# Half of the sequence-DFT sums made on the fly, other prepared sums moved to other units

## The chip, the core and the metric

The kernel runs on one core of one Trainium2 chip. A core has TensorE (PE, matrix products into PSUM), VectorE (DVE, elementwise), ScalarE (ACT, elementwise with a function), GpSimd (POOL) and SyncE (SP); each runs its own instructions in order, and they wait for each other by semaphores. SyncE and POOL also issue DMAs, which move data between the chip's memory (DRAM, here also used as scratch) and the on-chip pages. The metric is the time of one execution in microseconds of the device.

## The reference, cut to what matters

`x` is 2048 x 512, the sequence DFT matrices 2048 x 2048, the hidden ones 512 x 512, the gate and up weights 512 x 1792, the down weight 1792 x 512, all 32-bit floats.

```python
xn = _layernorm(x, axis=-1)
# FNet mixing, real part
a = einsum("bsd,ed->bse", xn, dft_hid_re)
b = einsum("bsd,ed->bse", xn, dft_hid_im)
s = einsum("ts,bse->bte", dft_seq_re, a) - einsum("ts,bse->bte", dft_seq_im, b)
# gated unit
h = sigmoid(xn @ w_gate) * (xn @ w_up)
g = silu(h @ w_down)
return x + s * g
```

## The kernel before, in words

**Products.** Each 32-bit operand is split into a hi part, rounded by ACT (line 67), and a lo part, the rest, by VectorE (line 68); a product is three matmuls, hi x hi, hi x lo, lo x hi (lines 71 to 73). Large products are made as 2 x 2 blocks in seven block products instead of eight, which needs sums and differences of the blocks ("sums" below) before and additions afterwards. The sums are VectorE operations recorded by one helper, `combine`, line 119.

**Order of work.** The program is a list of units, each a piece of TensorE work of some microseconds with the operands that it needs. A loop at the end (line 981 on) writes the instructions out unit by unit: the operations registered by `sooner(u, f)` ahead of unit u, the loads of the operands of units u to u+5 (`LOAD_AHEAD`), their splits for units u to u+2 (`SPLIT_AHEAD`), the unit's own work, then what `after(u, f)` registered. So the order on every engine and queue is fixed by unit numbers. All loads are issued by SyncE, nearly all stores by POOL. Data on the chip live in one pool of 53 pages of 4 KB per partition; a new page takes the place of one whose last use stands earlier in the program, and waits for that use.

**Stages.** The first half handles rows 0 to 1023 of `x`: a start, then blocks g = 1 to 6 of 256 hidden features each, nine units a block (`block_units`), units 0 to 53. The second half handles rows 1024 to 2047: block g = 0 in the same form (units 54 to 62), then six blocks in another form (`late_units`, seven units each). Then come the sequence DFT (`seq_units`) and the hidden DFT (`hidden_units`) with silu, product and addition of `x`. In the trace block 1 begins at 38.9 us, each block takes 30 to 31 us, the second half's first block begins at 222.2, the sequence DFT at 429.4, its four quarters of output rows at 429.4, 521.5, 597.7 and 673.8, the hidden DFT at 752.0.

**The sequence DFT.** A quarter has seven block products k in the order 1, 5, 6, 3, 7, 2, 4, each of four units pp = 0 to 3 with twelve matmuls of 512 columns. Units of this stage are numbered from its own start below (n in the code). Quarter 1 also carries eight small late down products of the gated unit, one behind every second unit, so it has units 0 to 35; quarter 2 has 36 to 63, quarter 3 has 64 to 91, quarter 4 has 92 to 119. The stationary operands are the blocks of `xn` (b11 etc. are the moving blocks of the DFT matrices, from `c_re` and `c_im`); split once in quarter 1, they stay on chip. Four of the moving operands of each pp are sums: t1 = b11 + b12 for k = 5, t2 = t1 + b22 for k = 6, t3 = b12 + b22 for k = 7, t4 = t2 + b21 for k = 4. In quarters 2 to 4 they are made during the quarter, the loads six units and the sum three units ahead of its use (line 844), in place in the block's page. In quarter 1 they are loaded from the scratch tensor `t_part`.

**Prepared sums.** `sums_ahead(n, make, blocks, to)` (line 675) loads four blocks ahead of units n and n+1 and, behind units n+3, n+5, n+6 and n+8, makes one sum each (VectorE, 128 x 1024) and stores it (POOL). It is used for
- `t_part`: the sums of quarter 1, pp = g - 1, in blocks g = 1 to 4 of the first half (line 961);
- `s_part`: differences of blocks of `xn`, rows 0 to 1023 in block 5 of the first half, rows 1024 to 2047 in the first block of the second half (line 963). `xn` itself is stored to `xn_part` as its row tiles are normalized; the last are stored behind unit 34;
- `w_part`: differences of the hidden DFT's weights `w_h`, from unit n+6 of the sequence DFT on (line 737).

**Silu ahead.** `silu_ahead(n, i)` (line 712), for i = 0 to 7, loads a page of the gated unit's output (`g_part` or `g_late`) ahead of unit n, makes the sigmoid on ACT behind unit n+2 (line 730), the product on VectorE behind n+3, and stores it to `gs_part`. The late down products end in accumulating stores to `g_late` (lines 460 and 462).

**After a product.** `snap` (line 795, ACT) copies a PSUM result out, `join` (line 802, VectorE) adds two, `two` makes four half-size sums of results, and POOL stores to `f_part`, which the hidden DFT reads.

Of the kernel before, what the change touches and what calls it, by code (L numbers as in the profile page):

```python
# [8 lines left out]
F32 = mybir.dt.float32  # L9
# [5 lines left out]
P = 128  # L15
S, D, F = 2048, 512, 1792
# [6 lines left out]
SB = 512  # L23
# [8 lines left out]
def fnet_glu_kernel(ctx: ExitStack, tc: tile.TileContext, x, c_re, c_im, w_h, w_gu, w_down, out):  # L32
# [6 lines left out]
    dram = ctx.enter_context(tc.tile_pool(name="dram", bufs=1, space=bass.MemoryType.DRAM))  # L39
# [21 lines left out]
    f_part = dram.tile([NT, 2, P, 8, SB], F32, name="f_part")  # L61
    w_part = dram.tile([4, P, 4, D // 2], F32, name="w_part")
    s_part = dram.tile([2, 4, P, 4, D // 2], F32, name="s_part")
    t_part = dram.tile([4, 4, P, 2, SB], F32, name="t_part")

    def split(hi, lo, src):
        nc.scalar.activation(hi, src, AF.Copy)  # L67
# [586 lines left out]
    def xn_blocks(q):  # L654
        a = {(d, j): Load(xn_part[q, j, d], [4, D // 2]) for d in range(2) for j in range(2)}
        return [a[k] for k in ((0, 0), (0, 1), (1, 0), (1, 1))]
# [76 lines left out]
    def seq_units(job):  # L733
        ops = a_operands()
        left = waiting + [(job, k) for k in SEVEN]
        n = len(units)
        sums_ahead(n + 6, diffs, [Load(w_h[i, j], [4, D // 2]) for i in range(2) for j in range(2)], w_part)
        for i in range(NS // 2):
            silu_ahead(n + 29 + 10 * i, i)
        for q in range(2):  # L740
            sooner(n - 5 + q, ops[1, q].load)
            sooner(n - 3 + q, ops[1, q].get)
        for tc_ in range(NT):
            n = len(units)
            bop = {}
            for pp in range(4):
                b11, b12, b21, b22 = c_blocks(tc_, pp)
                if tc_ == 0:
                    t1, t3, t2, t4 = (Load(t_part[pp, i], [2, SB]) for i in range(4))
                else:  # L750
                    t1 = Value([b11, b12], onto(b11.load, b12.load, ADD, nc.vector))
                    t2 = Value([b22], onto(t1.get, b22.load, ADD, nc.vector))
                    t3 = Value([b22], onto(b12.load, b22.load, ADD, nc.vector))
                    t4 = Value([b21], onto(t2.get, b21.load, ADD, nc.vector))
                bop[1, pp] = Parts([b11], b11.load, [2, SB])
                bop[5, pp] = Parts([t1], t1.get, [2, SB])
                bop[6, pp] = Parts([t2], t2.get, [2, SB])
                bop[3, pp] = Parts([b22], b22.load, [2, SB])
                bop[7, pp] = Parts([t3], t3.get, [2, SB])
                bop[2, pp] = Parts([b21], b21.load, [2, SB])  # L760
                bop[4, pp] = Parts([t4], t4.get, [2, SB])
                bop["t", pp] = {5: t1, 6: t2, 7: t3, 4: t4}
            ps, s, made = {}, {}, {}
            tags = {"a": "ab"[tc_ % 2], "b": "ba"[tc_ % 2], "c": "c"}

            def after_product(k, tc_=tc_, ps=ps, s=s, made=made):
                def halves(t):
                    return t.rearrange("p (h t) -> p h t", h=2)

                def put(blk):  # L770
                    half, j = blk // 2 ^ 1, blk % 2
                    nc.gpsimd.dma_start(f_part[tc_, half, :, 2 * j : 2 * j + 2, :], made[blk].rearrange("p h k t -> p h (k t)"))
                    if j == 0 or blk - 1 not in made:
                        return
                    (a0, a1), (b0, b1) = ([made[n][:, t, :, :].rearrange("p k t -> p (k t)") for t in range(2)] for n in (blk - 1, blk))
                    t1 = []

                    def two(i):
                        pg = page([2, SB], F32)
                        u, v = pg[:, 0, :], pg[:, 1, :]  # L780
                        if i == 0:
                            t1.append(combine(u, a0, a1, ADD))
                            combine(v, a1, b1, ADD)
                        else:
                            combine(u, t1[0], b1, ADD)
                            combine(v, u, b0, ADD)
                        nc.gpsimd.dma_start(f_part[tc_, half, :, 4 + 2 * i : 6 + 2 * i, :], pg)

                    after(now[0] + 1, lambda: two(0))
                    after(now[0] + 2, lambda: two(1))  # L790

                def snap(name, ch):
                    s[name] = page([2, 2, SB // 2], F32)
                    for d in range(2):
                        nc.scalar.activation(s[name][:, :, d, :], halves(ps[ch, d]), AF.Copy)
                    return s[name]

                def join(blk, name, ch, op, swap=False):
                    made[blk] = v = s[name]
                    for d in range(2):  # L800
                        x, y = v[:, :, d, :], halves(ps[ch, d])
                        nc.vector.tensor_tensor(v[:, :, d, :], *((y, x) if swap else (x, y)), op=op)
                    put(blk)

                if k == 1:
                    snap("u1", "a")
                elif k == 5:
                    snap("u5", "c")
                elif k == 6:
                    snap("u2", "a")  # L810
                elif k == 3:
                    join(2, "u2", "c", SUB)
                elif k == 7:
                    join(3, "u5", "a", SUB, swap=True)
                elif k == 2:
                    join(0, "u1", "b", ADD)
                else:
                    made[1] = snap("u4", "a")
                    put(1)

            CHAIN = {1: "a", 6: "a", 7: "a", 4: "a", 2: "b", 5: "c", 3: "c"}
            FIRST = (1, 2, 5)

            def run(k, pp, ops=ops, bop=bop, ps=ps, tags=tags, done=after_product):
                ch = CHAIN[k]
                if k in FIRST and pp == 0:
                    for d in range(2):
                        ps[ch, d] = bank("gu"[d] + tags[ch])
                wv, xv = ops[k, pp // 2].get(), bop[k, pp].get()
                for e in range(2):  # L830
                    o = 2 * (pp % 2) + e
                    for d in range(2):
                        ws = [t[:, o, d * P : (d + 1) * P] for t in wv]
                        first = k in FIRST and pp == e == 0
                        last = pp == 3 and e == 1
                        mm3(ps[ch, d], ws, [t[:, e, :] for t in xv], first, last, go_on=k not in FIRST)
                if pp == 3:
                    done(k)

            for k in ORDER:  # L840
                for pp in range(4):
                    m = len(units)
                    if tc_ and k in bop["t", pp]:
                        sooner(m - 6, bop["t", pp][k].load)
                        sooner(m - 3, bop["t", pp][k].get)
                    add([ops[k, pp // 2], bop[k, pp]], lambda k=k, pp=pp, run=run: run(k, pp))
                    if left and pp % 2:
                        last_down(*left.pop(0))
# [97 lines left out]
    with tc.manual_schedule():  # L946
# [3 lines left out]
        for h in range(NH):  # L950
            n = len(units)
            for g in range(NG):
                m = len(units)
                if h and g:
                    job = late_units(h, g, job)
                elif h:
                    job = block_units(h, g, job, [], Seven(g))
                elif g:
                    job = block_units(h, g, job, [])
                if h == 0 and 0 < g < 5:  # L960
                    sums_ahead(m, sums, c_blocks(0, g - 1), t_part[g - 1])
                elif (h, g) in ((0, 5), (1, 0)):
                    sums_ahead(m, diffs, xn_blocks(h), s_part[h])
            if h == 0:
                n = len(units)
                for i in range(KH):
                    m = 9 * (i // 2) + 6
                    if i % 2 == 0:
                        after(m - 6, lambda i=i: fetch(KH + i))
                    after(m - 4, lambda i=i: norm_a(KH + i))  # L970
                    after(m - 2, lambda i=i: norm_b(KH + i))
                    after(m, lambda i=i: (turn(KH + i), keep_raw(KH + i)))
                    after(m + 1, lambda i=i: store_xn(KH + i))
                for i, k in {-5: 1, -4: 2, 0: 6, 1: 5}.items():
                    sooner(n + i, xop[1, k].get)
                for i, k in {-3: 1, -2: 2, 1: 3, 2: 4}.items():
                    after(n + i, lambda k=k: x_sum(1, k))
            else:
                seq_units(job)
# [64 lines left out]
```

## Time and profile before

| | |
|---|---|
| median of three runs | 840.15 us (839.96 to 841.68) |
| the profiled execution | 840.49 us, span 838.6 us |
| TensorE busy | 822.7 us, 98% |
| VectorE busy | 656.9 us, 78% |
| ScalarE busy | 491.2 us, 59% |
| GpSimd busy | 145.6 us, 17% |
| DMA | 216.78 MB, mean 259 GB/s |
| granted TensorE clock | 1.00 |

A row of busy time names an engine, the sum of its instructions' time and its share of the span. In a list of waits, "PE gb L72 <- DVE page L68" is time in which TensorE stood still ahead of a matmul of line 72 until a VectorE operation of line 68 had ended; the numbers are the total, how often, and the longest. In a table by stretches, each row gives the stretch, its length, the busy time of each engine with its number of instructions, the granted clock, the mean busy share of the 16 DMA engines and what they moved. In a list of DMAs, "page<-t_part" is a load from `t_part` into a page; the last number is the median time from issue to landing.

### The profile page before, as it was taken

Reading aid. Unit: us, or ns where it says so; the run is one execution under the profiler, and the core shown is the slowest. Engines: PE = TensorE matmul, PEld = TensorE weight load, DVE = VectorE, ACT = ScalarE, POOL = GpSimd, SP = SyncE. Lnnn points to the kernel's source line nnn. Section 1 sums busy time; section 2 is a strip of 40 time slices with the busy share of each in tenths; the row PEclk is TensorE's granted clock in tenths of the full one; section 3 lists DMA queues with packets and bytes.
Section 4 is the critical chain, followed back from the end, with each engine's and each line's share of the span. In section 5 each row is a group of like instructions: output and inputs, shape, how many; then the busy total and the mean of one; then the engine's idle time right before and its main releaser. Section 6 shows DMA issues by size and latency. Waiting matters only on the chain.

```text
span 838.6 us, 11818 instructions
## 1 busy us (share of the span) xinstructions
PE 822.7 (98%) x4305; PEld 704.8 (84%) x4305; DVE 656.9 (78%) x850; ACT 491.2 (59%) x762; POOL 145.6 (17%) x222
## 2 busy tenths in 40 slices
PE   8899999999999999999999989999999999999997
PEld 7888888888877888888888868888888878889997
DVE  6798868766898867776796668968887878888875
ACT  4566655655667877777787655543455246444441
POOL 2143433321112112122121101001100110000100
PEclk9999999999999999999999999999999999999999
DMA  8359999989978989998999999636924983699951
GB/s 313 119 172 401 315 315 338 326 225 311 241 168 251 235 191 197 250 225 181 288 268 336 344 361 418 262 102 245 326 81 151 324 302 111 211 369 400 398 199 68
DMA packets 66155, 216.78 MB, mean 259 GB/s; under 512 B 6961, under 2 KB 7985, under 8 KB 66097
## 3 DMA queue, kind: packets, MB, share of 16 engines
q1 hardware_dynamic: 41280, 126.37, 41.3%
q0 software_dynamic: 24816, 89.66, 40.1%
q8 instruction: 33, 0.54, 0.3%
q14 instruction: 26, 0.20, 0.1%
HBM read 125.30 MB, written 90.70 MB: 258 GB/s over the span
## 4 chain that ended last, share of the span: by engine, by line
PE 83%; DVE 9%; issue 3%; DMA 3%; ACT 2%; POOL 0%; SPq 0%; DVEq 0%; ACTq 0%
PE pd L71 5%; PE pd L73 5%; PE pd L72 5%; PE ga L72 5%; PE ga L71 5%; PE ua L71 5%; PE ua L73 5%; PE ua L72 5%; PE ga L73 5%; DVE page L68 4%; PE gc L72 3%; PE uc L71 3%; PE uc L73 3%; PE gc L71 3%; PE uc L72 3%; PE gc L73 3%
## 5 line engine op out<-in xcount | busy, mean ns | idle before, releaser
L68 DVE TENSOR_TENSOR page<-page 128x1024 fp32r<-128x1024 f32 (+1 forms) x340 | 323.0, 979 | 129.8 <-ACT page L67 129.2
L67 ACT ACTIVATE page<-page 128x1024 fp32r<-128x1024 f32 (+1 forms) x340 | 277.9, 860 | 113.4 <-DVE page L119 79.3
L119 DVE TENSOR_TENSOR page<-page 128x512 f32<-128x512 f32 (+2 forms) x200 | 170.0, 872 | 1.0
L73 PE MATMUL pd<-page 128*128 128x256 f32 (+1 forms) x308 | 99.0, 321 | 0.0
L72 PE MATMUL pd<-page 128*128 128x256 f32 (+1 forms) x308 | 99.0, 321 | 0.0
L71 PE MATMUL pd<-page 128*128 128x256 f32 (+1 forms) x308 | 98.9, 321 | 0.0
L72 PE MATMUL ga<-page 128*128 128x512 f32 (+1 forms) x248 | 90.4, 364 | 1.6 <-DVE page L68 1.5
L71 PE MATMUL ga<-page 128*128 128x512 f32 (+1 forms) x248 | 90.4, 365 | 1.2 <-ACT page L309 0.8
L71 PE MATMUL ua<-page 128*128 128x512 f32 (+1 forms) x248 | 89.8, 362 | 1.1 <-DVE page L892 1.1
L73 PE MATMUL ga<-page 128*128 128x512 f32 (+1 forms) x248 | 89.8, 362 | 0.0
L73 PE MATMUL ua<-page 128*128 128x512 f32 (+1 forms) x248 | 89.7, 362 | 0.0
L72 PE MATMUL ua<-page 128*128 128x512 f32 (+1 forms) x248 | 89.7, 362 | 0.0
L458 ACT ACTIVATE page<-pd 128x512 f32<-128x512 f32 x98 | 57.4, 597 | 37.9 <-PE pd L73 32.8
L462 POOL DMA_DIRECT2D g_late<-page x45 | 38.7, 867 | 163.5 <-ACT page L458 113.1
L71 PEld LDWEIGHTS pd<-page 128*128 128x128 f32 x308 | 58.4, 190 | 6.8 <-ACT page L458 0.6
L72 PEld LDWEIGHTS pd<-page 128*128 128x128 f32 x308 | 58.4, 190 | 6.2
L73 PEld LDWEIGHTS pd<-page 128*128 128x128 f32 x308 | 58.4, 190 | 4.4
L72 PE MATMUL gc<-page 128*128 128x512 f32 (+1 forms) x148 | 54.5, 368 | 0.6 <-DVE page L68 0.6
L71 PE MATMUL gc<-page 128*128 128x512 f32 (+1 forms) x148 | 54.7, 370 | 0.0
L73 PE MATMUL gc<-page 128*128 128x512 f32 (+1 forms) x148 | 54.3, 367 | 0.0
L71 PE MATMUL uc<-page 128*128 128x512 f32 (+1 forms) x148 | 54.3, 367 | 0.0
L72 PEld LDWEIGHTS ga<-page 128*128 128x128 f32 x248 | 46.9, 189 | 8.7 <-DVE page L68 2.7
(136 smaller groups left out, 1501.8 us busy)
## 6 DMA issues: line engine op xcount, KB each, us to landing
g_late<-page POOLq DMA_DIRECT2D x49, 512.0 KB, 8.4
page<-in_c_re_dram SPq DMA_DIRECT2D x40, 512.0 KB, 6.7
page<-in_c_im_dram SPq DMA_DIRECT2D x36, 512.0 KB, 7.3
f_part<-page POOLq DMA_DIRECT2D x32, 512.0 KB, 6.7
page<-in_w_gu_dram SPq DMA_DIRECT2D x28, 512.0 KB, 7.0
g_part<-page POOLq DMA_DIRECT2D x28, 512.0 KB, 7.8
page<-f_part SPq DMA_DIRECT2D x28, 512.0 KB, 10.2
t_part<-page POOLq DMA_DIRECT2D x16, 512.0 KB, 9.0
```

Of the source, the lines that this page charges most:

```text
L67: nc.scalar.activation(hi, src, AF.Copy)
L68: nc.vector.tensor_tensor(lo, src, hi.bitcast(F32), op=SUB)
L71: nc.tensor.matmul(ps, ws[0], ms[0], start=first, stop=False, skip_group_check=go_on)
L72: nc.tensor.matmul(ps, ws[0], ms[1], start=False, stop=False, skip_group_check=go_on)
L73: nc.tensor.matmul(ps, ws[1], ms[0], start=False, stop=last, skip_group_check=go_on)
L119: (engine or nc.vector).tensor_tensor(dst, a, b, op=op)
L458: nc.scalar.activation(pg[:, 2 * i : 2 * i + 2, :], ps, AF.Copy, scale=float(sign))
L462: nc.gpsimd.dma_start(g_late[blk], pg, accum_op=ADD)
```

## The change

Five places change. `t_part` holds two sets in place of four, so blocks 3 and 4 of the first half make no DFT sums. In quarter 1 the units of pp = 0 and 1 still load their sums; those of pp = 2 and 3 make them on the fly in the way of the other quarters, from b11, b12, b22 and b21. The layernorm sums of rows 0 to 1023 are made in block 4 and those of rows 1024 to 2047 in block 5 of the first half. The weight sums start at unit 64 of the sequence DFT, the first of quarter 3, in place of unit 6. The silu steps start at units 28, 35, 42, 49, 56, 63, 70 and 77 in place of 29, 39, 49, 59, 69, 79, 89 and 99.

```diff
-    t_part = dram.tile([4, 4, P, 2, SB], F32, name="t_part")
+    t_part = dram.tile([2, 4, P, 2, SB], F32, name="t_part")
...
-        sums_ahead(n + 6, diffs, [Load(w_h[i, j], [4, D // 2]) for i in range(2) for j in range(2)], w_part)
+        sums_ahead(n + 64, diffs, [Load(w_h[i, j], [4, D // 2]) for i in range(2) for j in range(2)], w_part)
         for i in range(NS // 2):
-            silu_ahead(n + 29 + 10 * i, i)
+            silu_ahead(n + 28 + 7 * i, i)
...
-                if tc_ == 0:
+                if tc_ == 0 and pp < 2:
                     t1, t3, t2, t4 = (Load(t_part[pp, i], [2, SB]) for i in range(4))
...
-                    if tc_ and k in bop["t", pp]:
+                    if (tc_ or pp > 1) and k in bop["t", pp]:
                         sooner(m - 6, bop["t", pp][k].load)
                         sooner(m - 3, bop["t", pp][k].get)
...
-                if h == 0 and 0 < g < 5:
+                if h == 0 and g in (1, 2):
                     sums_ahead(m, sums, c_blocks(0, g - 1), t_part[g - 1])
-                elif (h, g) in ((0, 5), (1, 0)):
-                    sums_ahead(m, diffs, xn_blocks(h), s_part[h])
+                elif h == 0 and g in (4, 5):
+                    sums_ahead(m, diffs, xn_blocks(g - 4), s_part[g - 4])
```

## The prediction, made before the result was known

> **What bounds the kernel now.** I read the page's first table, then the waits of TensorE, then busy time stage by stage, then the first quarter's DMAs and what SyncE waits for there, and last the order of VectorE's work at a quarter's start.
>
> ```profile
> PE 822.7 (98%) x4305; PEld 704.8 (84%) x4305; DVE 656.9 (78%) x850; ACT 491.2 (59%) x762; POOL 145.6 (17%) x222
> ```
>
> TensorE is occupied for 98% of the span. In the stretches without a wait its 512-column matmuls start 0.227 us apart at a granted clock of 1.00, so a sequence unit of 12 takes 2.72 us. No TensorE work is removed; only its gaps can be won. Its waits (us in total, times, longest), and the stages (start:end, length, PE, PEld, DVE, ACT, POOL, PEclk, DMA share, GB/s):
>
> ```profile
> PE ga L72 <- DVE page L68: 1.5, 2, 0.8
> PE gb L72 <- DVE page L68: 1.2, 2, 0.8
> PE ga L71 <- ACT page L309: 0.8, 1, 0.8
> PE gb L73 <- DVE page L68: 0.6, 1, 0.6
> PE gc L72 <- DVE page L68: 0.6, 1, 0.6
> ```
>
> ```profile
> 222.20:253.50 31.30, 30.53 (x134) 24.54 (x133) 28.77 (x39) 20.34 (x34) 5.09 (x7) 1.00 0.79 196
> 429.40:521.50 92.10, 89.59 (x434) 74.41 (x433) 69.08 (x71) 59.66 (x75) 13.26 (x19) 1.00 1.04 355
> 521.50:597.70 76.20, 76.20 (x338) 63.09 (x337) 62.74 (x61) 35.88 (x40) 5.87 (x11) 1.00 0.61 228
> 597.70:673.80 76.10, 76.10 (x337) 63.03 (x336) 61.70 (x60) 34.66 (x39) 7.08 (x12) 1.00 0.60 209
> 673.80:752.00 78.20, 77.09 (x338) 62.87 (x337) 67.20 (x65) 39.57 (x44) 7.12 (x12) 1.00 0.69 241
> ```
>
> The rows are the first block of the second half, then the quarters of the sequence DFT. Quarters 2 and 3 take 28 x 2.72 = 76.2 us, nothing lost. Quarter 1 has eight late down products more (1.43 us each); its last three products, 12 units, ran from 484.8 to 521.5: 36.7 us against 32.6, so 4.0 us are lost, all after 484. Quarter 4 loses 2.0 (about 1.0 of it between 682 and 687). The first block takes 31.3 against 29.9 of the block before it, and the next one begins with waits of 0.3 and 0.8: 2.5 lost.
>
> Of quarter 1, its DMAs (count, size, median us from issue to landing), and what SyncE waited for:
>
> ```profile
> page<-t_part SPq DMA_DIRECT2D x14, 512.0 KB, 13.6
> page<-s_part SPq DMA_DIRECT2D x6, 512.0 KB, 16.4
> page<-in_w_h_dram SPq DMA_DIRECT2D x4, 512.0 KB, 12.8
> w_part<-page POOLq DMA_DIRECT2D x4, 512.0 KB, 12.6
> ```
>
> ```profile
> SPq L82 <- DMA w_part<-page: 16.9, 3, 8.1
> SPq L82 <- DMA g_late<-page: 14.8, 3, 8.8
> ```
>
> In quarter 1 the DMA engines are full throughout (1.04), a 512 KB load takes 13 to 16 us from issue to landing (5 to 6 us in quarters 2 and 3), and SyncE, which issues all loads in order, stood 16.9 us for pages that w_part stores still held. Those stores landed between 464 and 481; the loads behind them landed from 483 on, which is where TensorE begins to lose time. That stage is bound by late loads, not by VectorE (69 of 92 us). At a quarter's start it is VectorE:
>
> ```profile
> 606.53 1.22 DVE L68 TENSOR_TENSOR page<-page 128x1024 fp32r<-128x1024 f32 x1
> 607.66 1.22 DVE L119 TENSOR_TENSOR page<-page 128x1024 f32<-128x1024 f32 x1
> 608.80 1.22 DVE L68 TENSOR_TENSOR page<-page 128x1024 fp32r<-128x1024 f32 x1
> 609.93 1.22 DVE L119 TENSOR_TENSOR page<-page 128x1024 f32<-128x1024 f32 x1
> ```
>
> These are sums (L119) and lo halves (L68) in turn without idle time; each starts 1.137 us after the one before. The lo half begun at 606.53 ends at 607.75; TensorE starts that unit at 608.55 and needs it one matmul later: a lead of 1.0 us.
>
> **The change part by part.**
>
> First half. Eight DFT sums of blocks 3 and 4, with eight loads and eight stores, go; the layernorm sums of rows 0-1023 move from block 5 to 4, those of rows 1024-2047 from the second half's first block to 5. Blocks 1 to 6 show no TensorE wait, so what they save is worth 0. The added hazard: the four loads of xn_part's second half now follow its last stores, which landed at 168.2 and 169.5. SyncE stood at this place at 145.7 and will wait some 24 us there. Behind it are block 6's weights, issued at 161.9, then at about 171, landing about 179; they are wanted at about 184. Cost 0; if the loads land 7 us later still, 2 us.
>
> Second half's first block. It loses four loads, four stores and four sums of 1.22 us, begun at 240.69, 250.08, 251.33 and 258.95. Two of them directly precede the lo halves on which TensorE waits at 256.5 and 257.9 (0.3 and 0.8 us): 2.3 us of VectorE gone from a queue that is 1.1 us late. Gain 1.1; between 0 and 1.6. The wait on L309 at 231 lies before all four sums and stays.
>
> Quarter 1. Eight t_part loads go, two b12 loads come (b11, b22, b21 are loaded either way, b22 some seven units sooner); four w_h loads and four w_part stores go. That is 14 of about 65 transfers, 7.3 MB of 32.7 MB, or 20 us at 355 GB/s; and POOL's queue has no w_part stores between the g_late stores, so SyncE's 16.9 us go. VectorE gains eight sums and loses four: 4 x 1.14 = 4.6 us on 69 of 92. The sums are spread (at units 6, 7, 12, 13, 23, 24, 31, 32), and the fullest spot, units 31 to 35, keeps a lead of about 1 us (5.4 us between a product's end and the third unit after it, less two joins of 0.6, a silu product, a sum and a lo half of 1.14). I take 3.4 of the 4.0 us; bounds: 4.0, if no load is late, and -0.5, if none comes sooner and the sums' own load waits cost 0.5. What is new: VectorE stops at each sum until b12 or b22 has landed, with every lo half behind it; a b12 load issued at unit 3 at the old 18 us would stop it about 2 us.
>
> Silu steps, loads n+28+7i for n+29+10i. Each is a load, a sigmoid (1.05 on ACT), a product (1.14 on VectorE) and a 512 KB store. In quarter 4 none is left: its first sums lose the one of 677.69, and the waits at 682 and 687 (0.2 and 0.75) should go: gain 1.0, bounds 0 and 1.2. In quarter 2 step 1 moves from unit 42 to 38, into a run where each unit has 2.72 us for one sum and one lo half (2.27): the lead 1.0 + 0.45 - 1.14 = 0.3 holds. Cost 0, at most 0.5.
>
> Quarter 3 gets the weight sums after units 67, 69, 70, 72 and the silu product after 66. Its lead by the unit, from 1.0 at unit 68: 69: +0.45 - 1.14 = 0.3; 70: -0.35; then from 0: 71: 0.45; 72: -0.24; 73: -0.69; 74: 0.45; from 75 on there are no sums and it recovers. TensorE waits 0.35 + 0.24 + 0.69 = 1.3 us. Bounds: 0, since quarter 2's start kept VectorE full (20.96 of 21 us) without a wait, and 5: 1.3 plus about 4, if one operand's page is still held by a w_part store (landing 7 us after its sum, where an operand has some 3).
> [...]
>
> SyncE, POOL and ACT elsewhere: quarter 3 has room (DMA share 0.60, POOL 7.1 of 76.1 us) for four loads and four stores; w_part's readers come in quarter 4 and gs_part's after 752, both later than the new stores. Cost 0; without that room, later loads as in quarter 1, within the 5 above.
>
> Sum: 840.5 - 1.1 - 3.4 - 1.0 + 1.3 = 836.3. The profiled execution took 840.49 us (span 838.6 plus 1.9 around it), 0.3 above the median of 840.15; I leave that.
>
> **The rivals.**
>
> A: quarter 1's loads stay late. SyncE also waited 14.8 us there for pages of g_late stores, which stay, and VectorE now stops for b12. Against it: a fifth of the bytes go. With a third of the gain, 1.1, the time is 838.6; with none, 839.7.
> [...]
>
> B, on the other side: quarter 3's page wait. By lifetimes read from the code, of 53 pages at most 50 are live there now, and up to 52 with the weight blocks and an earlier silu step. If sums, operands and loads take pages whose stores have not landed, each costs 3 to 4 us. Two of them (+8) with the gains as forecast give 843; from 5.5 us lost in quarter 3 the change is slower than no change, from 7.2 by over 0.2%. Against it: in quarter 2's like start ACT and VectorE show no wait for a store.
>
> C: the gaps are merely shifted, each gain met by a new wait of its size: 840.
>
> **How the numbers follow.** A run tells 0.2% (1.7 us) from no change: below 838.5 is faster, above 841.8 slower. Forecast (834 to 838.4) 0.64; A 0.14, of which 0.04 below 838.5; C 0.08; B 0.14. Faster 0.64 + 0.04 = 0.68; same 0.10 + 0.08 = 0.18; slower 0.14. The lowest sum is 840.5 - 1.6 - 4.0 - 1.2 = 833.7, unlikely in full, so 834.2; the upper end takes in A and most of C: 840.4.
>
> **What would show it.** Right: quarter 1 about 89 us long, its DMA share below 1, loads landing within 10 us, no SyncE wait for w_part; the waits at 256 to 258 gone, the one on L309 left; quarter 3 about 77.5 us with TensorE waiting on L68 near its sixth to tenth unit; quarter 4 about 77.2. Wrong: quarter 1 still over 91 us, VectorE idle there before L119 for a load, or quarter 3 above 81 us with ACT or VectorE waiting for a w_part, gs_part or f_part store.

## The result, and the profile after

The changed kernel takes 835.63 us (median of 6 runs, 835.39 to 836.37) against 840.06 us before (median of 6): ratio 0.9944, 95% interval 0.9931 to 0.9956. That is 0.56% faster; 836.3 was forecast, in a range of 834.2 to 840.4. Its profiled execution has a span of 833.2 us against 838.6.

The page's first table of the changed kernel. TensorE's busy time fell by 2.6 us, for the same matmuls, since a pause counts in part as busy: before, the matmul at 484.83 is recorded with 0.49 us and the next one begins 1.26 us later, for 0.23 without a pause, of which 0.77 are listed as a wait.

```profile
PE 820.1 (98%) x4305; PEld 704.9 (85%) x4305; DVE 655.7 (79%) x850; ACT 490.1 (59%) x762; POOL 140.3 (17%) x214
```

Stage by stage (start:end, length, PE, PEld, DVE, ACT, POOL, granted clock, DMA share, GB/s), after the change: the second half's first block, the four quarters of the sequence DFT.

```profile
222.00:253.10 31.10, 30.34 (x134) 24.62 (x133) 27.21 (x39) 22.41 (x38) 3.40 (x4) 1.00 0.78 203
427.40:516.00 88.60, 88.15 (x435) 74.47 (x434) 72.97 (x75) 58.34 (x75) 10.98 (x15) 1.00 1.00 309
516.00:592.10 76.10, 76.10 (x337) 63.04 (x336) 63.79 (x62) 36.67 (x41) 7.25 (x13) 1.00 0.61 218
592.10:669.70 77.60, 76.97 (x337) 62.82 (x336) 67.11 (x65) 35.55 (x40) 10.68 (x18) 1.00 0.73 272
669.70:746.60 76.90, 76.45 (x337) 62.98 (x337) 64.83 (x63) 37.66 (x42) 4.26 (x8) 1.00 0.61 216
```

Lengths, each from the first matmul of a stage to the first of the next (the stage of all second-half blocks goes to the start of quarter 1):

| stage | before | after | change | forecast |
|---|---|---|---|---|
| first half, blocks 1 to 6 | 183.3 | 183.3 | 0 | 0 |
| second half, all blocks | 207.2 | 205.3 | -1.9 | -1.1 |
| quarter 1 | 92.1 | 88.6 | -3.5 | -3.4 |
| quarter 2 | 76.2 | 76.2 | 0 | 0 |
| quarter 3 | 76.2 | 77.6 | +1.45 | +1.3 |
| quarter 4 | 78.15 | 76.9 | -1.25 | -1.0 |
| hidden DFT | 86.6 | 86.5 | -0.1 | 0 |

Quarter 1's loads after the change (count, size, median us from issue to landing), then SyncE's waits in quarter 1:

```profile
page<-t_part SPq DMA_DIRECT2D x6, 512.0 KB, 9.3
page<-s_part SPq DMA_DIRECT2D x7, 512.0 KB, 7.0
```

```profile
SPq L82 <- DMA g_late<-page: 28.6, 4, 9.9
SPq L82 <- DVE page L68: 13.9, 10, 3.9
```

These two kinds of load land in 9.3 and 7.0 us (medians) where they took 13.6 and 16.4. The 16.9 us of waits for w_part stores are gone, but SyncE now stands longer for g_late stores, 28.6 us for 14.8, and TensorE does not notice. That is the first sign that SyncE's waits were not what cost the time.

VectorE's order at quarter 3's start after the change (start, length, idle before):

```profile
600.99 1.22 DVE L68 TENSOR_TENSOR page<-page 128x1024 fp32r<-128x1024 f32 x1
602.13 2.36 DVE L119 TENSOR_TENSOR page<-page 128x1024 f32<-128x1024 f32 x2
604.40 1.22 DVE L68 TENSOR_TENSOR page<-page 128x1024 fp32r<-128x1024 f32 x1
605.53 2.35 DVE L119 TENSOR_TENSOR page<-page 128x1024 f32<-128x1024 f32 x2
607.81 1.22 DVE L68 TENSOR_TENSOR page<-page 128x1024 fp32r<-128x1024 f32 x1
```

Where one sum stood between two lo halves there are now two: at 602.13 the silu product beside a DFT sum, at 605.53 the first weight sum. The lo half of unit 70 ends at 609.03; TensorE had begun that unit at 608.45, and its second matmul starts at 609.08.

### The profile page after: what moved, and what is told of

It reads as the page before. It is cut to its first block, busy times and chain, and to the rows that moved or that the text cites. A ratio compares the mean times of both kernels' runs of the same rounds, so it can differ in the third digit from the quotient of the medians.

```text
span 833.2 us, 11773 instructions
## 1 busy us (share of the span) xinstructions
PE 820.1 (98%) x4305; PEld 704.9 (85%) x4305; DVE 655.7 (79%) x850; ACT 490.1 (59%) x762; POOL 140.3 (17%) x214
## 4 chain that ended last, share of the span: by engine, by line
PE 85%; DVE 8%; issue 2%; DMA 2%; ACT 2%; SPq 0%; DVEq 0%
PE pd L73 6%; PE pd L72 6%; PE pd L71 6%; PE ga L72 5%; PE ua L71 5%; PE ga L71 5%; PE ua L73 5%; PE ua L72 5%; PE ga L73 5%; DVE page L68 4%; PE gc L71 3%; PE gc L72 3%; PE uc L71 3%; PE uc L73 3%; PE uc L72 3%; PE gc L73 3%
## 5 line engine op out<-in xcount | busy, mean ns | idle before, releaser
L71 PE MATMUL ua<-page 128*128 128x512 f32 (+1 forms) x248 | 89.8, 362 | 1.1 <-DVE page L892 1.1
L73 PE MATMUL ga<-page 128*128 128x512 f32 (+1 forms) x248 | 89.8, 362 | 0.0
L71 PE MATMUL uc<-page 128*128 128x512 f32 (+1 forms) x148 | 54.3, 367 | 0.0
L73 PE MATMUL uc<-page 128*128 128x512 f32 (+1 forms) x148 | 54.2, 366 | 0.0
```

The lines of the kernel that those rows point to most:

```text
L71: nc.tensor.matmul(ps, ws[0], ms[0], start=first, stop=False, skip_group_check=go_on)
L73: nc.tensor.matmul(ps, ws[1], ms[0], start=False, stop=last, skip_group_check=go_on)
```

## The experiments

Two questions were open. Quarter 1: fewer bytes (the theory of bytes), or SyncE no longer held by pages that w_part stores kept (the theory of the hold)? And the rest: is each gain and loss VectorE's queue, at the place forecast? Lengths below are those of the profiled execution of each run. Behind each time stands its ratio to the kernel before, measured beside it, with the 95% interval. A passage set off behind an edit is what was expected before that run.

**Undoing one part: the weight sums (w_back).**

```diff
-        sums_ahead(n + 64, diffs, [Load(w_h[i, j], ...
+        sums_ahead(n + 6, diffs, [Load(w_h[i, j], ...
```

> The changed kernel with the weight sums back at unit 6. Two theories of quarter 1, which became 3.5 us shorter (92.1 to 88.6). Bytes: 14 transfers fewer relieve the DMA engines, each its share; 8 of the 14 come back, so quarter 1 takes 90.6. Hold: SyncE stood for pages that w_part stores held, so all of it comes back, 92.1. Both: quarter 3 loses its VectorE queue and takes 76.4 for 77.6. Time: bytes 836.4, hold 837.9, against 835.6 of the changed kernel.

836.41 us (0.9944, 0.9924 to 0.9963). Quarter 1 took 90.6, quarter 3 76.2. (Its profiled execution began block 1 at 41.2 us, 2.4 later than the others, in a start that is the same in all kernels; so stages are compared. Of its four executions two took 835.2 and 835.5 us, two 837.4 and 837.9.) Time and quarter 1 are the numbers that the theory of bytes gave, but by luck. TensorE pauses twice in this quarter 1, at unit 34 as in the changed kernel, and for 1.74 us at unit 15 (466.34). VectorE's order ahead of that:

```profile
457.64 1.22 DVE L68 TENSOR_TENSOR page<-page 128x1024 fp32r<-128x1024 f32 x1 [0.80 <-ACT page L67]
458.79 2.35 DVE L119 TENSOR_TENSOR page<-page 128x1024 f32<-128x1024 f32 x2
461.06 0.68 DVE L68 TENSOR_TENSOR page<-page 128x512 fp32r<-128x512 f32 x1
461.66 2.35 DVE L119 TENSOR_TENSOR page<-page 128x1024 f32<-128x1024 f32 x2
463.93 3.48 DVE L68 TENSOR_TENSOR page<-page 128x1024 fp32r<-128x1024 f32 x3
```

Behind units 11 and 12 a weight sum now stands beside each DFT sum. The lo half at 457.64 begins 27.94 us after the stage's start, exactly as in the changed kernel (455.30); from there VectorE works without a pause, and two sums more, 2 x 1.14 us, make the second of the three lo halves late. So the 2.0 us that quarter 1 lost against the changed kernel are VectorE's queue, and no load's lateness is in them.

**Undoing one part: the DFT sums (t_back).**

```diff
-    t_part = dram.tile([2, 4, P, 2, SB], F32, name="t_part")
+    t_part = dram.tile([4, 4, P, 2, SB], F32, name="t_part")
...
-                if tc_ == 0 and pp < 2:
+                if tc_ == 0:
...
-                    if (tc_ or pp > 1) and k in bop["t", pp]:
+                    if tc_ and k in bop["t", pp]:
...
-                if h == 0 and g in (1, 2):
+                if h == 0 and 0 < g < 5:
...
-                elif h == 0 and g in (4, 5):
+                if h == 0 and g in (4, 5):
```

> The changed kernel with all four sets of DFT sums made ahead again (in blocks 1 to 4) and loaded in quarter 1; weight sums, silu and layernorm sums stay as changed. Bytes: 6 of the 14 transfers of quarter 1 come back, +1.5, and VectorE's wait of 0.6 at unit 34 goes, so 89.5. Hold: no w_part store is there, quarter 1 takes 88.0. The first half costs nothing in both. Time: bytes 836.5, hold 835.0.

835.40 us (0.9935, 0.9921 to 0.995). Quarter 1 took 87.9: no loss at all, with eight t_part loads more (and two b12 loads fewer) and no sums in it. So quarter 1's gain does not need the DFT sums made on the fly; as made here, together with the silu product behind unit 31 (silu_back below), they cost it 0.75. The first half took 184.1 for 183.3, in short pauses at 170.6, 184.6 and 193.9 us, that is in blocks 5 and 6. Block 4, just ahead of them, makes two sets of sums in this kernel; that these make the pauses was not tested. Both theories had put the first half at nothing.

**The kernel before, without four stores (no_w_store).**

```diff
-            nc.gpsimd.dma_start(to, at)
+            if store:
+                nc.gpsimd.dma_start(to, at)
...
-        v1, v3, v2, v4 = (Load(w_part[i], [4, D // 2]) for i in range(4))
+        v1, v3, v2, v4 = (Load(w_h[i, j], [4, D // 2]) for i in range(2) for j in range(2))
```

This kernel leaves out the use of the differences: its hidden DFT reads plain weight blocks in their place, with the same loads and matmuls, and returns other numbers.

> The kernel before, with the weight blocks loaded and summed at unit 6 as before, but not stored; the hidden DFT loads the plain weight blocks in place of their differences, so its five difference products are of other numbers, with the same loads and matmuls. Only the four w_part stores go from quarter 1. Bytes: 4 of 14 transfers less, quarter 1 takes 91.1 for 92.1. Hold: SyncE's 16.9 us of waits go with them, quarter 1 takes 88.7. Time: bytes 839.1, hold 836.7, against 840.1 before.

836.64 us (0.9951, 0.9936 to 0.9966). Quarter 1 in this kernel:

```profile
429.50:517.40 87.90, 87.90 (x435) 74.60 (x434) 68.92 (x71) 58.98 (x75) 11.02 (x15) 1.00 1.04 352
```

Four stores fewer, 2.1 MB of 32.7, win 4.2 us, and the DMA share is still 1.04. Loads of c_re still take 14.7 us from issue to landing. It looked like the theory of the hold.

**The changed kernel with eight useless loads (more_loads).**

```diff
+        for i, u in enumerate((4, 5, 10, 11, 21, 22, 29, 30)):
+            sooner(n + u, Load(t_part[i // 4, i % 4], [2, SB]).load)
```

> The changed kernel with eight loads of 512 KB that nobody reads, issued in quarter 1 at the units at which the dropped t_part loads stood. Bytes: 8 of the 14 transfers are back, quarter 1 takes 90.6 for 88.6. Hold: loads without a store or a reader hold no page for long, quarter 1 stays at 88.6. Time: bytes 837.6, hold 835.6.

835.87 us (0.9942, 0.9927 to 0.9956). Quarter 1 took 88.6 again. Eight loads cost nothing, so a price per byte is refuted.

**The changed kernel with four useless stores (more_stores)** where the w_part stores had been, from a page that stays in use:

```diff
+    d_part = dram.tile([4, P, 4, D // 2], F32, name="d_part")
...
+        for i, u in enumerate((9, 11, 12, 14)):
+            after(n + u, lambda i=i: nc.gpsimd.dma_start(d_part[i], ops[1, 0].get()[0].bitcast(F32)))
```

> The changed kernel with four stores of 512 KB from a page that stays in use anyway, to a scratch tensor that nobody reads, behind units 9, 11, 12 and 14, where the w_part stores stood. Hold (a page that waits for its store keeps SyncE standing): no page is released by them, quarter 1 stays at 88.6. Traffic (the written bytes, or four more stores in POOL's queue ahead of the g_late stores): quarter 1 goes back to 91 or 92. Time 835.6 or 838 to 839.

835.67 us (0.9947, 0.9933 to 0.9962), quarter 1 88.6. Stores by themselves cost nothing either, as the hold had it.

**The kernel before, with the hold alone taken away (w_kept).**

```diff
             nc.gpsimd.dma_start(to, at)
+            if keep:
+                after(keep, lambda: nc.vector.tensor_copy(stat.tile([P, 1], F32, name="last"), at[:, 0, :1]))
...
-        sums_ahead(n + 6, diffs, [Load(w_h[i, j], ... w_part)
+        sums_ahead(n + 6, diffs, [Load(w_h[i, j], ... w_part, keep=n + 44)
```

> The kernel before with all its work in place, but the four pages of the weight sums are each read once more behind unit 44 (one column, VectorE), so that none of them is free while its w_part store is under way. Hold: quarter 1 takes 87.9 for 92.1, the time is 836. Traffic of the stores, or their place in POOL's queue: quarter 1 stays at 92, the time 840.

840.03 us (0.9998, 0.9989 to 1.0008): no difference. Quarter 1 of this kernel, and SyncE's longest waits in it:

```profile
429.40:521.20 91.80, 89.30 (x434) 74.33 (x433) 68.93 (x71) 59.40 (x75) 13.22 (x19) 1.00 1.04 354
```

```profile
SPq L82 <- DMA g_late<-page: 27.4, 4, 13.1
SPq L82 <- DMA page<-t_part: 12.1, 8, 3.1
```

The wait for w_part stores is gone; SyncE waits for g_late stores in its place, 27.4 us for 14.8, and everything lands when it did: the first xn_part load of the stage 64.0 us after its start, for 64.2 before. Keeping four of the 53 pages could by itself make SyncE wait for others, so this run alone does not settle it. The run with eight loads does: SyncE stood there 45.7 us for g_late stores in quarter 1, against 28.6 in the changed kernel and 14.8 before, and no time was lost. So the theory of the hold falls. Both theories are out as they were stated, the bytes by more_loads, the hold by these two runs.

**A budget.** Put side by side, quarter 1 of the kernels fits one rule, with one row that says nothing on it. The bytes and rates are those that the trace gives for the stretch of quarter 1.

| kernel | MB | GB/s | MB / 355 GB/s | quarter 1 |
|---|---|---|---|---|
| before | 32.7 | 355 | 92.1 | 92.1 |
| before, w pages kept | 32.5 | 354 | 91.6 | 91.8 |
| weight sums back | 31.9 | 352 | 89.8 | 90.6 |
| before, no w stores | 31.0 | 352 | 87.2 | 87.9 |
| eight loads more | 30.6 | 345 | 86.1 | 88.6 |
| DFT sums back | 30.2 | 344 | 85.2 | 87.9 |
| four stores more | 29.4 | 332 | 82.9 | 88.6 |
| changed | 27.4 | 309 | 77.1 | 88.6 |

Quarter 1 takes the longer of two times: TensorE's own, 87.9 (88.6 with the VectorE wait at unit 34, explained below), and the time in which the DMA engines move its bytes at about 355 GB/s. Before, it was the second, by 4.2 us; by this rule taking 1.5 MB away wins all of it (no_w_store took 1.7), less wins a part, and nothing beyond that wins more. The row that says nothing is that of the weight sums back: what it lost is VectorE's, as shown above. The five kernels not in the table moved 26.4 to 30.1 MB and took 87.9 or 88.6. The 355 GB/s are the mean of this mix of transfers, at a full DMA share: before, the thirds of quarter 1 moved 324, 341 and 401 GB/s; why they differ was not looked into. The rule was formed after the fact, and a longer stage also counts more bytes, so it was put to a test with a forecast of its own: sixteen useless loads (the run sixteen).

```diff
+        for i, u in enumerate((4, 5, 6, 7, 9, 10, 11, 12, 14, 16, 18, 20, 21, 22, 24, 26)):
+            sooner(n + u, Load(t_part[i // 4 % 2, i % 4], [2, SB]).load)
```

> The changed kernel with sixteen loads of 512 KB that nobody reads, between units 4 and 26 of quarter 1. Budget theory, formed from the runs so far: quarter 1 takes the longer of TensorE's own 87.9 us and its bytes at about 355 GB/s, the rate at which it ran in the kernel before; the change left 27.4 MB there, well below the 31 MB that 87.9 us hold. Sixteen loads add 8.4 MB, some 35 MB in all, so quarter 1 takes 95 to 101 us and the time is 842 to 848. If the gain came only from what SyncE waits for, stores that hold pages, these loads cost nothing, as eight did: 88.6 and 835.6.

844.97 us (1.0054, 1.0037 to 1.0071). Quarter 1:

```profile
427.10:526.60 99.50, 92.29 (x433) 75.26 (x433) 73.26 (x75) 59.26 (x75) 10.99 (x15) 0.98 1.04 360
```

35.8 MB in 99.6 us, 360 GB/s. Eight such loads cost 0, sixteen cost 11.0 us (9.3 by the medians of the times). ScalarE's splits stood 22 us for loads that had not landed, none of it in the changed kernel. The budget holds; some 1.4 us of the 99.6 are matmuls at half speed (last section). What stays open: nearly all transfers here are of 512 KB, and a useless load also takes a page until it has landed, so bytes, number of transfers and pages are not told apart. That this stage moved the most bytes per microsecond of all speaks for the bytes.

**One VectorE product more behind unit 66 (one_more).**

```diff
+            if i == 5:
+                combine(page([2, D], F32), t.get(), g.load(), ALU.mult)
             v = combine(t.get(), t.get(), g.load(), ALU.mult)
```

> The changed kernel with one VectorE product of 128x1024 more, made behind unit 66 beside silu's own and not used. Queue theory: at quarter 3's start VectorE is behind by what is put in, so quarter 3 takes 1.14 us more, 78.7 for 77.6. If instead a page or a load is what TensorE waits for there, quarter 3 stays at 77.6. Time 836.8 or 835.6.

836.26 us (0.9957, 0.9942 to 0.9972). Quarter 3 took 78.9, that is 1.3 more, for 1.14 forecast. TensorE's waits in quarter 3 (total, times, longest), first of the changed kernel, then of this one:

```profile
PE ga L72 <- DVE page L68: 0.4, 1, 0.4
PE gc L72 <- DVE page L68: 0.2, 1, 0.2
```

```profile
PE gc L72 <- DVE page L68: 1.2, 2, 0.8
PE ga L72 <- DVE page L68: 0.4, 1, 0.4
```

The added operation appears as TensorE's wait for a lo half, nearly one for one. ScalarE stood once for a gs_part store (1.9 us at 612.3), and TensorE's listed waits are all for VectorE's lo halves.

**Undoing one part: the silu steps (silu_back).**

```diff
-            silu_ahead(n + 28 + 7 * i, i)
+            silu_ahead(n + 29 + 10 * i, i)
```

> The changed kernel with the silu steps back at units 29, 39 and so on. Queue theory: quarter 3 loses the silu product behind unit 66 and keeps the four weight sums: 76.5 for 77.6. Quarter 4 has its silu product at unit 92 back: 78.1 for 76.9. Quarter 1 has its product one unit later, behind the lo halves of unit 34: 88.0 for 88.6. If the weight sums alone make quarter 3's wait, it stays at 77.6. Time 835.1, or 836.2.

835.10 us (0.9942, 0.9926 to 0.9959). Quarter 1 took 87.9, quarter 3 76.7, quarter 4 78.15, each within 0.2 of the queue theory. Of quarter 3's 1.45 us the weight sums alone make 0.55, the silu product behind unit 66 the rest; quarter 4's gain is the silu steps' whole gain; the product behind unit 31, beside the DFT sums made on the fly, cost quarter 1 its 0.75. On balance the silu move wins nothing as made: -1.25 + 0.9 + 0.75 is a loss of 0.4 us in these lengths, and the times of the two kernels (0.9942 and 0.9944) do not tell them apart.

**Undoing one part: the layernorm sums (xn_back).**

```diff
-                elif h == 0 and g in (4, 5):
-                    sums_ahead(m, diffs, xn_blocks(g - 4), s_part[g - 4])
+                elif (h, g) in ((0, 5), (1, 0)):
+                    sums_ahead(m, diffs, xn_blocks(h), s_part[h])
```

> The changed kernel with the layernorm sums where they were: rows 0 to 1023 in block 5, rows 1024 to 2047 in the second half's first block. Queue theory: the four VectorE sums there make TensorE wait at four places again, so quarter 1 begins 1.5 us later, and nothing else moves: 837.2. If the second half's gain of 1.9 came from the lighter DMA load of the first half, it stays: 835.6.

837.17 us (0.9967, 0.9954 to 0.998). The second half took 207.2 again. TensorE's waits between 222 and 270 us in this kernel, of which the changed one has only the first:

```profile
PE ga L71 <- ACT page L309: 0.8, 1, 0.8
PE gb L73 <- DVE page L68: 0.6, 1, 0.6
PE gb L71 <- ACT page L67: 0.2, 1, 0.2
```

So the four sums there, with their loads and stores, cost 1.9 us, and the lighter DMA load of the first half gives none of it.

**One number changed in the kernel before (w_only):** the weight sums at unit 64.

```diff
-        sums_ahead(n + 6, diffs, [Load(w_h[i, j], ...
+        sums_ahead(n + 64, diffs, [Load(w_h[i, j], ...
```

> The kernel before with one number changed: the weight sums start at unit 64. Hold: quarter 1 takes 87.9, with all four sets of DFT sums loaded; quarter 3 takes 76.7, as with the silu steps at their old units; quarter 4 stays at 78.1 and the second half's first block as before. Time 836.4. If the DFT sums made on the fly are needed for quarter 1's gain, it takes 89.5 or more.

836.90 us (0.9959, 0.9945 to 0.9974). Quarter 1 took 87.9, quarter 3 76.7, the rest as before. This one line is three quarters of the change's gain (the ratio is 0.4% of its 0.56%).

**A better version (tuned).** VectorE's extra work goes, but for one weight sum (behind unit 78), to units where no DFT sum is made, and the hidden weights are split ahead of such units too.

```diff
-        sums_ahead(n + 64, diffs, ...
+        sums_ahead(n + 70, diffs, ...
-            silu_ahead(n + 28 + 7 * i, i)
+            silu_ahead(n + (42, 44, 50, 52, 59, 71, 79, 87)[i], i)
...
-                sooner(n - 26 + 5 * i, v.load)
-                sooner(n - 22 + 5 * i, w[k].get)
+                at = n - (18, 17, 16, 11, 10)[i]
+                sooner(at - 4, v.load)
+                sooner(at, w[k].get)
```

> The changed kernel with VectorE's extra work put where a unit has no sum of its own: the weight sums start at unit 70 (made behind units 73, 75, 76, 78), the silu steps at 42, 44, 50, 52, 59, 71, 79, 87, and the hidden weights are split ahead of units 102, 103, 104, 109, 110 in place of 98, 103, 108, 113, 118. Queue theory: quarter 1 87.9, quarters 2, 3 and 4 76.2 each, so 833.0. If pages or loads take over as the limit there, quarter 2 or 3 grows by a microsecond or more and the time is 835 or above.

832.40 us: 0.9906 of the time before, 0.9891 to 0.992, faster than both kernels. Its four quarters:

```profile
427.80:515.60 87.80, 87.80 (x433) 74.53 (x433) 71.83 (x74) 57.45 (x74) 10.45 (x14) 1.00 0.99 301
515.60:591.80 76.20, 76.20 (x338) 63.10 (x337) 65.28 (x63) 37.76 (x42) 7.65 (x14) 1.00 0.62 222
591.80:668.10 76.30, 76.30 (x337) 62.99 (x336) 67.48 (x65) 36.00 (x40) 10.80 (x19) 1.00 0.73 265
668.10:744.30 76.20, 76.20 (x338) 63.10 (x337) 64.67 (x63) 37.67 (x42) 4.29 (x8) 1.00 0.67 238
```

PE busy equals the length in each: quarter 3 keeps 0.2 us of loss, the others none. VectorE does 67.5 us in quarter 3, 0.4 more than in the changed kernel's 77.6 us stage.

## Why the prediction was right, and where it was not

- First half, 0: right. SyncE stood for xn_part stores in two waits of 42.3 us together, longest 29.1 (24 forecast), and VectorE once for 6.6 us; TensorE not at all.
- Second half's first block: the mechanism was right, the size was off, 1.9 for 1.1 and outside its bound of 1.6. The term counted two waits, 0.3 and 0.8 us. Beside the kernel with these sums put back, four places of the changed kernel are shorter: at 248.5 us by 0.2, at 256.6 by 0.4, at 258.0 by 0.9 and at 264.7 by 0.3. Two of them are pauses too short for the list of waits, and the other two each cost 0.1 more than was counted: in the traces of the kernels before and after the step from the 512-column matmul that ends a pause to the next takes 0.33 or 0.34 us for 0.23, unless it is a pause itself. The wait on L309 stayed, as said.
- Quarter 1: -3.5 for -3.4, but the reason was half right. The step "so SyncE's 16.9 us go" was taken as a cause, and w_kept shows that it is none. What is right is that the stage was bound by DMA; it is a limit with a knee, not a share for each transfer (eight loads more cost 0, sixteen 11.0 us), and each of two edits alone gets below it: the weight sums moved (w_only) or their stores left out. The sign named for it, a DMA share below 1, did not come (1.00 at 309 GB/s, 1.04 at 345 without any loss): the share does not tell a full stage from one with room. Bytes over the rate at which the full stage ran did so here.
- The fullest spot, units 31 to 35: the step "keeps a lead of about 1 us" failed. The terms in its own bracket give 0.8, and the queue was counted without the lo halves of the stationary operands, which quarter 1 also splits; one more lo half of 1.14 us makes of the lead a wait, 0.6 us as measured, at unit 34, whose second matmul starts at 510.63, when the second of three lo halves has ended:

```profile
505.95 2.35 DVE L119 TENSOR_TENSOR page<-page 128x1024 f32<-128x1024 f32 x2
508.22 3.49 DVE L68 TENSOR_TENSOR page<-page 128x1024 fp32r<-128x1024 f32 x3
```

The end of the late loads won 4.2 us, and this wait, with the step behind it, took 0.75; that the sum's 3.4 came close is chance.
- Silu and quarter 4: -1.25 for -1.0, bound 1.2; two pauses went, and the step behind each was not counted. Quarter 2: 0, as forecast.
- Quarter 3: +1.45 for +1.3, with the waits at units 70, 72 and 73, where the lead table had put them: 0.5, 0.2 and 0.7 us with the step behind each, for 0.35, 0.24 and 0.69 in the table. The table with VectorE's step of 1.137 us was right; with 1.22, the duration that the trace records for a single sum, the same table gives 2.5 us.
- Rival A (loads stay late) was wrong here; late loads come back only near the old traffic, 3.9 us at 32.5 MB and none at 31.0. The three stages that lost time to late loads (those of the kernel before, of w_kept and of sixteen) ran at 354 to 360 GB/s, though the last 22.5 us of quarter 1 before moved 419. Rival B (page waits in quarter 3): ScalarE stood once for an f_part store in the changed kernel, 1.4 us at 603.65, VectorE worked on without a pause, and TensorE waited for lo halves alone. C (each gain met by a new wait of its size) did not come.

## What to carry to other kernels

Before moving a transfer, divide the stage's bytes by the rate at which the full stage ran, compare it with the other engines' own time, and expect back only what lies above that: here 32.7 MB at 355 GB/s, 92.1 us, against TensorE's 87.9. That is shown here for one stage and one mix of transfers. A long wait in an issue queue was no cause by itself in this case: with the 16.9 us for w_part stores taken away, SyncE waited 12.6 us longer for g_late stores, and the time stayed (840.03 us, 0.9998). Where an in-order engine alternates between two operations that take nearly all of the time that the consumer gives it, here 2.27 of 2.72 us a unit, count every operation unit by unit, and put extra work where the alternation pauses: here that took quarter 3 from 77.6 to 76.3 us.

## What was not expected of the hardware

In the run with sixteen loads TensorE waited 2.23 us for one lo half, and the matmuls behind it ran at half speed for a while: starts 0.43 us apart for seven of them, for 0.23 otherwise. The trace records a granted clock of 0.5 from 520.11 for 3.41 us.

```profile
519.65 0.50 PE L72 MATMUL ga<-page 128*128 128x512 f32 x1 [2.23 <-DVE page L68]
...
521.16 0.63 PE L73 MATMUL ua<-page 128*128 128x512 f32 x1
521.59 0.63 PE L71 MATMUL ga<-page 128*128 128x512 f32 x1
522.01 0.63 PE L72 MATMUL ga<-page 128*128 128x512 f32 x1
```

This wait cost TensorE more than itself, some 1.4 us (seven times 0.2). The length of the wait alone does not decide it. In w_back the clock stayed full behind the wait of 1.74 us at unit 15, but in its start a wait of 1.40 us, up to 13.85, was followed by the same granted clock of 0.5, from 14.04 for 3.41 us; in the kernels before and after the clock is 1.00 from 10 to 20 us, and their longest waits between 10 and 16 us are 0.69 and 0.71 us. This stretch, with the longer wait, is where w_back's block 1 became late. What decides it is not shown.
